# 29 semaphores instead of 48: signals between two engines share a counter, in a cached-attention decode kernel

## The chip, the cores and the metric

The kernel runs on one core of one Trainium2 chip. A time is the device time of one execution in microseconds; "before" is the median of three executions. The profile is one further execution with the hardware profiler on.

## What is computed

One decode step for two sequences (B = 2, one query each, D = 512), as a gated sum of attention and an MLP:

```
xn  = layernorm(x)                                   # x = A_x [2, 1, 512]
s   = attention(xn): q = xn @ wq (32 heads of 128), k_cache / v_cache [2, 8, 32768, 128],
      p = softmax(q.k * 128**-0.5), o = p @ v, s = o @ wo
g   = silu(B(xn)):  h = gelu(layernorm(xn) @ w1), four shifted slices of h @ w2,
      x1 = xn + (that), h2 = gelu(layernorm(x1) @ w3) @ w4, x1 + h2
out = x + s * g
```

With a sequence length of one the four shifted slices hold only padding, so w1 and w2 contribute nothing, and the kernel does not read them. What remains to be read is the K and V caches, 2 x 8 x 32768 x 128 bf16 each, 134 MB each, and some 12 MB of weights: 280.5 MB by the profile.

## The kernel before

**The work.** There are 16 *groups*, one for each sequence and KV head. A group's K and V are 8.39 MB each, laid out as 128 partitions of 256 keys. `kbuf` has three slots of half a group, `vbuf` two. For a group, VectorE transposes K in 16 pieces into the four buffers `T` (L558); TensorE multiplies each with the query matrix `z` into the score banks `sc` (L664). After eight pieces the first half of the scores is complete. VectorE takes row maxima (`mx`, `mxr`, L537 to L541), TensorE spreads them (`S`, L676), VectorE reduces them to `shift` (L569), ScalarE takes the exponential into `ep` (L478), VectorE transposes that into `pt` (L577), TensorE multiplies it with V into `o` (L687), ScalarE copies `o` to `ob` (L483). The division by the sum of a group is put off into the next group: TensorE adds up the four parts (`oT`, L624), VectorE divides (`head_on`: `den`, `rec`, `recm`, `on`, L513 to L522), TensorE turns the result (`xp`, L630), VectorE reduces it (`head_out`, L528 to L534) to `oXs`, GpSimd copies that to its place in `oX` (`put_o`, L498) and makes the next `z` (`put_z`, L491). The prologue (layernorms, q, the MLP) comes ahead of the groups; at the end come the products with `wo` (L703 to L748), `sg` = s * g (L614), `out` = x + sg (L615), and two stores (L617).

**The order.** Every engine has one queue, written out by hand. VectorE's loop body holds two groups and runs 8 turns, TensorE's holds one and runs 16, GpSimd and ScalarE have their own loops. SyncE issues all large loads in a fixed order without a loop: wq, w3, w4, K of group 0, V of group 0, then for each m the K of group m (L442), released when TensorE begins the last of the first eight pieces of group m - 1, and V of group m (L427), released when ScalarE sees the last product with V of group m - 1. After the last V come six pieces of `wo` (`wo_parts`, L457 to L466), each with a semaphore of its own (`d_wo`).

**The signals.** Outside the loops a semaphore only grows, and a `Queue` object (L27) notes which value each step waits for: `s_ve`, `s_ac`, `s_po`, `s_pe` are the engines' own counters. In the loops a signal is either *taken*, with a wait that also subtracts (`take`, L468, its row on line 469: one instruction of the sequencer), or, on VectorE, awaited as a growing count and subtracted at the end of the turn: the object `c` (`Counts`) keeps, for each semaphore, how many a turn has used, and L583 to L584 then take those totals. In front of a turn's end these are ten semaphores: `t_z`, `t_k0`, `t_used`, `t_k1`, `t_d`, `t_S`, `t_oT`, `t_xp`, `t_top`, `t_e`. `t_used` says that TensorE is done with a T buffer, `t_T` that a T piece is there, `t_mx`, `t_pt`, `t_on` that the operands of L676, L687 and L630 are there, `t_sm` and `t_oX` signal to GpSimd, `s_half`, `s_pv` release K and V loads, `s_oX` counts GpSimd's copies. An instruction carries one wait itself; a further one is a separate instruction in front of it.

**The end.** After the last store has landed, the engines meet in a barrier, GpSimd clears the range of semaphores that the program allocated (L779), and a second barrier follows. The kernel allocates 42 of the 48, the frame around it six.

Of the kernel before, what the change touches and what calls it, by code (L numbers as in the profile page):

```python
# [11 lines left out]
ALU = mybir.AluOpType  # L12
# [9 lines left out]
T_BUFS = 4  # L22
# [96 lines left out]
def kernel(  # L119
# [140 lines left out]
    d_x, d_x4, d_wq, d_w3, d_w4, d_g, d_out = (  # L260
        sem(f"d_{n}") for n in ("x", "x4", "wq", "w3", "w4", "g", "out")
    )
    d_wo = [sem(f"d_wo{i}") for i in range(len(wo_parts))]
    t_T, t_z, t_mx, t_pt, t_ob, t_on = (sem(f"t_{n}") for n in ("T", "z", "mx", "pt", "ob", "on"))
    t_used, t_top, t_e, t_S, t_oT, t_xp = (sem(f"t_{n}") for n in ("used", "top", "e", "S", "oT", "xp"))
    t_d, t_shift, t_pv, t_sm, t_oX = (sem(f"t_{n}") for n in ("d", "shift", "pv", "sm", "oX"))
    t_k = [sem(f"t_k{i}") for i in range(NPART)]
    t_v = [sem(f"t_v{i}") for i in range(NPART)]
    s_half, s_pv, s_oX = (sem(f"s_{n}") for n in ("half", "pv", "oX"))
# [19 lines left out]
    with tc.tile_critical(sync_engine=mybir.EngineType.Pool, no_gpsimd_drain=True):  # L289
# [25 lines left out]
        ve.op(lambda e: e.memset(S[:, 0:NPART * rep], 1.0), inc=(t_S, 1))  # L315
# [117 lines left out]
        load_v(0, e_h2)  # L433
        for n in range(NQ):
            sp.op(lambda v, n=n: v.dma_start(out=g4[32 * n:32 * n + B, :], in_=g[:, n * QW:(n + 1) * QW]), e_g, e_g0, inc=(d_g, 16))
# [3 lines left out]
        for m in range(1, NG):  # L439
            base = m % 2  # L440
            if m < NG - 1:
                sp.op(lambda e, m=m, base=base: e.dma_start(  # L442
                    out=kbuf[:, base * SLOT:(base + NPART) * SLOT], in_=row_view(A_k_cache, *groups[m])),
                    (s_half, m), e_q, inc=(t_k[0], 16))
            else:
                for i, h in enumerate(order(m)):
                    sp.op(lambda e, m=m, h=h, base=base: e.dma_start(
                        out=kbuf[:, (base + h) * SLOT:(base + h + 1) * SLOT],
                        in_=row_view(A_k_cache, *groups[m])[:, h * SLOT:(h + 1) * SLOT]),
                        (s_half, m), inc=(t_k[i], 16))  # L450
            load_v(m, (s_pv, m))
        for i, (a, c, r0, r1) in enumerate(wo_parts):
            cols = slice(r0 * D, r1 * D)
            if i == LOW:
                rows = wos[:, a, cols]
                for p in range(4):
                    sp.op(lambda e, p=p, rows=rows: e.dma_start(  # L457
                        out=wo_low[LQ + p:LQ + LP:4, 0:2, :],
                        in_=rows[0:2 * LP, :].rearrange("(u p) c -> p u c", u=2)[p:LP:4, :, :]), (s_pv, NG - 1), inc=(d_wo[i], 16))
                    sp.op(lambda e, p=p, rows=rows: e.dma_start(  # L460
                        out=wo_low[LQ + p:LQ + LOW_N[2]:4, 2, :], in_=rows[2 * LP + p::4, :]), (s_pv, NG - 1), inc=(d_wo[i], 16))
                continue
            if i == 0:
                sp.op(lambda e, c=c: e.dma_start(out=kbuf[:, 0:RW * D], in_=A_wo[0:128 * RW, :].rearrange("(p r) d -> p (r d)", r=RW)), (s_pv, NG - 1), inc=(d_wo[i], 16))  # L464
                continue
            sp.op(lambda e, a=a, c=c, cols=cols: e.dma_start(out=wo3[:, a:c, cols], in_=wos[:, a:c, cols]), (s_pv, NG - 1), inc=(d_wo[i], 16))  # L466
# [5 lines left out]
        ac.op(lambda v: v.activation(out=warm[:, :], in_=ones_f[:, 0:1], func=ACT.Exp), e_ones)  # L472
        with nc.Fori(0, NG // 2, engines=[ACTE]):
            for par in range(2):
                take(nc.scalar, t_shift)
                for h in range(NPART):
                    i = order(par).index(h)
                    nc.scalar.activation(  # L478
                        out=ep[i][:, :], in_=sc[i][:, :], func=ACT.Exp, scale=inv_sqrt_dh, bias=shift[:, :],
                        accum_out=rs[:, i:i + 1]).then_inc(t_e, 1)  # L480
                take(nc.scalar, t_pv)
                nc.scalar.sem_inc(s_pv, 1)  # L482
                nc.scalar.copy(out=ob[:, :], in_=o[:, :]).then_inc(t_ob, 1)  # L483

# [11 lines left out]
        def put_o(m):  # L496
            take(nc.gpsimd, t_oX)
            nc.gpsimd.tensor_copy(out=oX[:, bass.ds(m, 1), :].rearrange("p m r -> p (m r)"), in_=oXs[:, :]).then_inc(s_oX, 1)  # L498
# [5 lines left out]
        with nc.Fori(0, NG - 1, engines=[POOL]) as m:  # L504
            put_o(m)
            take(nc.gpsimd, t_sm)
            put_z(m + 1)
        put_o(NG - 1)
        e_oX = [(s_oX, m + 2) for m in range(NG - 1)] + [None]


        def head_on(c, last=False, between=None):
            nc.vector.tensor_reduce(  # L513
                out=den[:, :], in_=S[:, 0:NPART * rep].rearrange("p (i h) -> p h i", h=rep),
                axis=AX.X, op=ALU.add).wait_op(*c(t_S), "sem-ge").then_inc(*c.inc(t_d))
# [6 lines left out]
            ins = nc.vector.tensor_mul(  # L522
                out=on[:, :, :], in0=oT[:, :].unsqueeze(1).broadcast_to([128, NQ, rep]), in1=recm[:, :, :]).wait_op(*c(t_oT, 2), "sem-ge")
            if last:
                ins.then_inc(t_on, 1)

        def head_out(c, last=False):
            nc.vector.tensor_mul(  # L528
                out=xm[:, :, :], in0=xp_b[:, :].rearrange("p (r h) -> p r h", r=NQ),
                in1=mask[:, :].unsqueeze(1).broadcast_to([128, NQ, rep])).wait_op(*c(t_xp), "sem-ge").then_inc(*c.inc(t_d))  # L530
            with nc.allow_low_precision(reason="three of the four terms are zero, the fourth is bf16"):
                if last:
                    return ve.op(lambda v: v.tensor_reduce(out=oX[:, NG, :], in_=xm[:, :, :], axis=AX.X, op=ALU.add), c.at(t_d))
                nc.vector.tensor_reduce(out=oXs[:, :], in_=xm[:, :, :], axis=AX.X, op=ALU.add).wait_op(*c.at(t_d), "sem-ge").then_inc(t_oX, 1)  # L534

        def peak(c, i, *event):
# [5 lines left out]
            if i == NPART - 1:  # L542
                ins.then_inc(t_mx, 1)

        nc.br("dve_groups", engines=[DVE])
        with nc.body("dve_groups", valid_engines=[DVE]):
            c = Counts()
            for par in range(2):
                nc.vector.wait_ge(*c(t_z))
                for i, h in enumerate(order(par)):  # L550
                    u = par + h
                    kt = kbuf[:, u * SLOT:(u + 1) * SLOT].bitcast(I32)
                    for r in range(NR):
                        n = i * NR + r
                        events = ([c(t_k[i], 16)] if r == 0 else []) + ([c(t_used)] if n >= T_BUFS else [])
# [7 lines left out]
                        ins.then_inc(t_T, 1)  # L563
                        if i == 1 and r == 3:
                            peak(c, 0)
                            head_on(c)
                head_out(c)
                peak(c, 1, *c(t_used, T_BUFS))
                nc.vector.tensor_reduce(  # L569
                    out=shift[:, :], in_=S[:, NPART * rep:], axis=AX.X, op=ALU.min).wait_op(*c(t_top), "sem-ge").then_inc(t_shift, 1)  # L570
                for h in range(NPART):
                    e = c(t_e)
                    if h == NPART - 1:
                        nc.vector.tensor_mul(
                            out=sm[:, :, :], in0=sel_h[:, :].unsqueeze(1).broadcast_to([128, NPART, rep]),
                            in1=rs[:, :].unsqueeze(2).broadcast_to([128, NPART, rep])).wait_op(*e, "sem-ge").then_inc(t_sm, 1)
# [5 lines left out]
                    ins.then_inc(t_pt, 1)  # L582
# [11 lines left out]
        e_wd, e_mv, e_ws, e_s = ((pe.sem, pe.n + i) for i in (1, 2, 3, 4))  # L594
# [19 lines left out]
        e = ve.op(lambda v: v.tensor_tensor(out=sg[0:QP, :], in0=pro[0:QP, 0:QW], in1=g4[0:QP, :], op=ALU.mult), (d_g, 16 * NQ), e_s)  # L614
        e = ve.op(lambda v: v.tensor_tensor(out=out4[0:QP, :], in0=sg[0:QP, :], in1=x4_bf[0:QP, :], op=ALU.add), (d_x4, 16 * B), e)  # L615
        for b, q in ((0, sp), (1, ac)):
            q.op(lambda v, b=b: v.dma_start(out=out[b, 0, :].rearrange("(n c) -> n c", c=QW), in_=out4[b:QP:32, :]), e, inc=(d_out, 16))  # L617
        sp.wait((d_out, 32))


        def head_oT():
# [5 lines left out]
            ins.then_inc(t_oT, 1)  # L627

        def head_xp():
            nc.tensor.matmul(  # L630
                xp_b[:, :], lhsT=sel_w[:, :, :].rearrange("p j w -> p (j w)"), rhs=on[:, :, :].rearrange("p r h -> p (r h)"),
                start=True, stop=True).then_inc(t_xp, 1)
# [12 lines left out]
        pe.n, pe.seen = prologue.n, prologue.seen  # L645
# [6 lines left out]
        with nc.body("pe_groups", valid_engines=[PE]):  # L652
            for i in range(NPART):
                for r in range(NR):
                    pairs = i == 0 or r < 4
                    if not pairs:
                        take(nc.tensor, t_T)
                    elif r % 2 == 0:
                        take(nc.tensor, t_T, 2)
                    Tb = Ts[(i * NR + r) % T_BUFS][:, :].bitcast(BF16).rearrange("p (b c e) -> p b c e", b=NB, e=2)  # L660
                    zc = (NR - 1 - r) * rep
                    for nb in range(NB):
                        for w in range(2):
# [4 lines left out]
                            if i == 0 and r == NR - 1 and nb == 0 and w == 0:  # L668
                                ins.then_inc(s_half, 1)
                    ins.then_inc(t_used, 1)  # L670
# [4 lines left out]
            take(nc.tensor, t_mx)  # L675
            nc.tensor.matmul(  # L676
                S[:, NPART * rep:], lhsT=same_h[:, :], rhs=mxr[:, :, :].rearrange("p i r -> p (i r)"),
                start=True, stop=True).then_inc(t_top, 1)
            for h in range(NPART):
                fill(FILL[h])  # L680
                take(nc.tensor, t_v[h], 16)
                take(nc.tensor, t_pt)
# [13 lines left out]
                start=True, stop=True).then_inc(t_S, 1)  # L696
# [4 lines left out]
        with nc.body("pe_output", valid_engines=[PE]):  # L701
# [7 lines left out]
            take(nc.tensor, t_on)  # L709
            head_xp()  # L710
            for i in (0, 2, LOW, 3, 4, 5):
# [13 lines left out]
                for k in range(a, c):  # L725
                    pe.wait(e_oX[(B - 1) * Hkv + k], (d_wo[i], 16 * (8 if i == LOW else 1)), *((e_low, e_low0) if i == LOW else (e_wide,) if i == 0 else ()))
# [57 lines left out]
```

## Time and profile before

| | |
|---|---|
| three executions | 656.88, 657.32, 658.47 us; median 657.32 us |
| profiled execution, its own time | 656.51 us |
| span, first to last instruction | 654.7 us |
| TensorE, matmul | 431.4 us busy, 66% |
| VectorE | 379.5 us, 58% |
| ScalarE / GpSimd | 39.7 us / 14.2 us, 6% / 2% |
| DMA queue of SyncE | 280.50 MB, 99.1% of 16 engines' span |

"PE" is TensorE, "PEld" its weight load, "DVE" VectorE, "ACT" ScalarE, "POOL" GpSimd, "SP" SyncE; a name with q is that engine's sequencer. The span is the time from the first to the last instruction; the 1.81 us by which the execution's own time is longer lie around it. Semaphore instructions do not count as busy, but they appear as rows of a line.

### The profile page before, as it was taken

The page shows a single profiled execution, that of the slowest core. Times are in us where ns is not written, and L with a number is a line of the kernel's source. Part 1 is how long each engine was busy: PE and PEld are TensorE (multiplying, and loading weights), DVE is VectorE, ACT ScalarE, POOL GpSimd, SP SyncE. Part 2 cuts the span into 40 slices and gives each one's busy share as a digit, 9 for nine tenths or more (in the row PEclk, how much of TensorE's full clock was granted, in tenths as well). Part 3 has the DMA queues.
Part 4 walks back from the last instruction along what each step waited for, and adds up shares of the span by engine and source line. Part 5 has one row for each costly group of instructions (what it writes and reads, how often), then busy time and mean ns, then how long its engine had stood idle before and what let it go on. Part 6 is the DMA issues. An engine that isn't in the chain of part 4 may idle for free. (4 is left out here: it accounts for less than half of the span.)

```text
span 654.7 us, 6536 instructions
## 1 busy us (share of the span) xinstructions
PE 431.4 (66%) x2568; PEld 163.6 (25%) x2568; DVE 379.5 (58%) x538; ACT 39.7 (6%) x90; POOL 14.2 (2%) x45
## 2 busy tenths in 40 slices
PE   2438487583958748395783839668384875838886
PEld 0013132231313213131321313222131322313332
DVE  5348193673919457292855819276481936639681
ACT  1200001000010100001000000100001010000100
POOL 1200000000000000000000000000000000000000
PEclk9759789696997969789796978969697796969999
DMA  8999999999999999999999999999999999998997
GB/s 366 435 449 449 445 392 445 440 448 396 444 440 448 440 400 444 444 448 392 448 440 448 416 424 444 444 448 392 448 440 448 416 424 444 444 448 388 448 416 292
DMA packets 6314, 280.54 MB, mean 428 GB/s; under 512 B 798, under 2 KB 936, under 8 KB 1448
## 3 DMA queue, kind: packets, MB, share of 16 engines
q1 hardware_dynamic: 6300, 280.50, 99.1%
q8 instruction: 2, 0.03, 0.0%
q10 hardware_dynamic: 12, 0.00, 0.0%
HBM read 280.50 MB, written 0.00 MB: 428 GB/s over the span
## 5 line engine op out<-in xcount | busy, mean ns | idle before, releaser
L558 DVE STREAM_TRANSPOSE T<-kbuf 128x1024 int32<-128x1024 int32 x256 | 294.8, 1211 | 202.9 <-DMA kbuf<-in_A_k_cache_dram 196.3
L664 PE MATMUL sc<-T,z 128*128 128x512 bf16 x1024 | 277.7, 420 | 176.1 <-PEq L469 172.7
L664 PEld LDWEIGHTS sc<-T,z 128*128 128x128 bf16 x1024 | 98.0, 104 | 339.4 <-issue 258.8
L687 PE MATMUL o<-vbuf,pt 128*16 128x512 bf16 x1024 | 78.8, 380 | 7.3 <-PEq L469 4.4
L637 PE MATMUL pro<-ob,comb 128*2 128x512 f32 x130 | 61.1, 592 | 0.0
L478 ACT ACTIVATE ep<-sc,shift 128x512 bf16<-128x512 f32 x32 | 21.7, 682 | 485.5 <-ACTq L469 485.5
L687 PEld LDWEIGHTS o<-vbuf,pt 128*16 128x16 bf16 x1024 | 27.2, 88 | 55.3 <-issue 33.2
L577 DVE STREAM_TRANSPOSE pt<-ep 128x512 bf16<-128x512 bf16 x32 | 22.7, 708 | 15.0 <-ACT ep L478 15.0
L537 DVE TENSOR_REDUCE mx<-sc 128x1 f32<-128x512 f32 x32 | 21.5, 672 | 15.8 <-PE sc L664 15.8
L676 PE MATMUL S<-mxr,same_h 128*128 128x64 f32 x32 | 6.5, 285 | 18.4 <-PEq L469 18.4
L624 PEld LDWEIGHTS oT<-sel_o,ob 128*128 128x128 f32 x136 | 17.7, 191 | 3.2 <-issue 0.5
L637 PEld LDWEIGHTS pro<-ob,comb 128*2 128x2 f32 x130 | 9.6, 84 | 26.8 <-issue 21.9
L624 PE MATMUL oT<-sel_o,ob 128*128 128x4 f32 x136 | 16.2, 242 | 0.0
L483 ACT COPY ob<-o 128x512 f32<-128x512 f32 x16 | 9.4, 585 | 96.4 <-ACTq L469 96.4
L498 POOL COPY oX<-oXs 128x4 bf16 (+1 forms) x16 | 3.0, 186 | 527.5 <-POOLq L469 527.5
L676 PEld LDWEIGHTS S<-mxr,same_h 128*128 128x128 f32 x32 | 4.8, 188 | 26.2 <-issue 26.2
L569 DVE TENSOR_REDUCE shift<-S 128x1 f32<-128x64 f32 x16 | 3.6, 224 | 9.4 <-PE S L676 9.4
L541 DVE TENSOR_SCALAR mxr<-row_of,mx 128x32 f32<-128x32 f32 x32 | 7.7, 242 | 1.1
L694 PEld LDWEIGHTS S<-sm,ones_f 128*128 128x128 f32 x32 | 5.0, 195 | 6.9 <-issue 6.9
L491 POOL TENSOR_TENSOR z<-qr,quad 128x64 bf16<-128x64 bf16 x16 | 4.7, 293 | 80.6 <-POOLq L469 65.6
L694 PE MATMUL S<-sm,ones_f 128*128 128x8 f32 x32 | 6.4, 273 | 0.0
L372 PE MATMUL qrb<-ident,xs_bf 34*128 34x34 bf16 x4 | 0.3, 193 | 9.1 <-DVE xs_bf L337 9.1
(103 smaller groups left out, 82.0 us busy)
## 6 DMA issues: line engine op xcount, KB each, us to landing
kbuf<-in_A_k_cache_dram SPq DMA_DIRECT2D x2, 4096.0 KB, 22.6
vbuf<-in_A_v_cache_dram SPq DMA_DIRECT2D x2, 4096.0 KB, 22.5
kbuf<-in_A_wq_dram SPq DMA_DIRECT2D x1, 4096.0 KB, 12.3
vbuf<-in_B_w_dram SPq DMA_DIRECT2D x2, 1792.0 KB, 17.9
kbuf<-in_A_wo_dram SPq DMA_DIRECT2D x1, 2048.0 KB, 31.5
kbuf<-in_A_wo_dram SPq DMA_DIRECT2D x3, 512.0 KB, 26.3
shared<-in_A_wo_dram SPq DMA_DIRECT2D x4, 66.0 KB
kbuf<-in_A_k_cache_dram SPq DMA_DIRECT2D x15, 27.4
```

The costliest lines, as they stand in the source:

```text
L478: nc.scalar.activation(out=ep[i][:, :], in_=sc[i][:, :], func=ACT.Exp, scale=inv_sqrt_dh, bias=shift[:, :], accum_out=rs[:, i:i + 1]).then ...
L483: nc.scalar.copy(out=ob[:, :], in_=o[:, :]).then_inc(t_ob, 1)
L537: ins = nc.vector.tensor_reduce(out=mx[:, i:i + 1], in_=sc[i][:, :], axis=AX.X, op=ALU.max)
L541: ins = nc.vector.tensor_scalar_mul(out=mxr[:, i, :], in0=row_of[:, :], scalar1=mx[:, i:i + 1]).wait_op(*c.at(t_d), "sem-ge")
L558: ins = nc.vector.transpose(out=Ts[n % T_BUFS][:, :].rearrange("p (b t k) -> p t b k", b=NB, t=RT), in_=kt[:, r * W:(r + 1) * W].rearrange ...
L577: ins = nc.vector.transpose(out=pt[h][:, :, :].rearrange("p r (t h) -> p t r h", h=rep), in_=ep[order(par).index(h)][:, :].rearrange("p (t ...
L624: ins = nc.tensor.matmul(oT[:, :], lhsT=ob[:, t * Dh:(t + 1) * Dh], rhs=sel_o[:, t, :], start=(t == 0), stop=(t == VT - 1))
L637: nc.tensor.matmul(pro[0:B, :], lhsT=comb[:, :], rhs=ob[:, :], start=True, stop=True)
L664: ins = nc.tensor.matmul(sc[i][:, :], lhsT=z[:, nb, w, zc:zc + 128], rhs=Tb[:, nb, :, w], start=(r == 0 and nb == 0 and w == 0), stop=(r = ...
L676: nc.tensor.matmul(S[:, NPART * rep:], lhsT=same_h[:, :], rhs=mxr[:, :, :].rearrange("p i r -> p (i r)"), start=True, stop=True).then_inc( ...
L687: ins = nc.tensor.matmul(o[32 * j:32 * j + VT * rep, :], lhsT=pt[h][:, r, a * VT * rep:(a + 1) * VT * rep], rhs=vt[:, u * VT:(u + 1) * VT, ...
L694: nc.tensor.matmul(S[:, 0:NPART * rep], lhsT=ones_f[:, :], rhs=sm[:, :, :].rearrange("p i h -> p (i h)"), start=True, stop=True).then_inc( ...
```

## The change

The same signals are carried by fewer counters; every computing instruction, load and store stays, in the same order.

- VectorE to TensorE: `t_T`, `t_mx`, `t_pt`, `t_on` become `t_vt`. VectorE to GpSimd: `t_sm`, `t_oX` become `t_vg`.
- TensorE to VectorE: `t_used`, `t_top`, `t_S`, `t_oT`, `t_xp` become `t_tv`. A group has 20 such signals in a fixed order, and VectorE waits for places in it (`used`, `sum_of`, `out_of`, `turned`); a turn's end subtracts 40.
- `recm`, which signalled `t_oT` beside TensorE, signals `t_d`, so that `on` now has two waits, one of them separate.
- `s_half`, `s_pv`, `s_oX` become further counts of `s_pe`, `s_ac`, `s_po`; `s_sp`, which nothing used, goes.
- The six `wo` pieces and the stores count on in the prologue's `d_wq`, `d_w3`, `d_w4`, `d_x`, `d_x4`, `d_g`.

A turn's end on VectorE now subtracts six semaphores: `t_z`, `t_k0`, `t_k1`, `t_d`, `t_e`, `t_tv`.

```diff
-    sp = Queue(nc.sync, sem("s_sp"))
+    sp = Queue(nc.sync, None)
...
+    d_wo = [d_wq, d_w3, d_w4, d_x, d_x4, d_g]
+    n_wo = [16, 16, 16, 16, 16 * B, 16 * NQ]
+    for i in range(len(wo_parts)):
+        n_wo[i] += 16 * (8 if i == LOW else 1)
+    d_out, n_out = d_wq, n_wo[0] + 16 * B
+    t_vt, t_vg, t_tv = (sem(f"t_{n}") for n in ("vt", "vg", "tv"))
+    t_z, t_ob, t_e, t_d, t_shift, t_pv = (sem(f"t_{n}") for n in ("z", "ob", "e", "d", "shift", "pv"))
...
-                    (s_half, m), e_q, inc=(t_k[0], 16))
+                    (pe.sem, pe_0 + m), e_q, inc=(t_k[0], 16))
...
-            load_v(m, (s_pv, m))
+            load_v(m, (ac.sem, ac_0 + m))
...
-        ac.op(lambda v: v.activation(out=warm[:, :], in_=ones_f[:, 0:1], func=ACT.Exp), e_ones)
+        ac.op(lambda v: v.activation(out=warm[:, :], in_=ones_f[:, 0:1], func=ACT.Exp), e_ones, inc=False)
...
+        N_T = NPART * NR + 4
+        def used(par, n):
+            return t_tv, par * N_T + n + 2 + (n >= NR) + (n >= NR + 5)
+        def sum_of(par):
+            return t_tv, par * N_T + 1
+        def out_of(par, last=False):
+            return t_tv, par * N_T + (2 if last else NR + 2)
+        def turned(par, last=False):
+            return t_tv, par * N_T + (3 if last else NR + 8)
...
-                in1=sel_h[:, :].unsqueeze(2).broadcast_to([128, NQ, rep])).wait_op(*c.at(t_d), "sem-ge").then_inc(t_oT, 1)
+                in1=sel_h[:, :].unsqueeze(2).broadcast_to([128, NQ, rep])).wait_op(*c.at(t_d), "sem-ge").then_inc(*c.inc(t_d))
+            e = c.at(t_d)
             if between:
                 between()
+            nc.vector.wait_ge(*out_of(par, last))
             ins = nc.vector.tensor_mul(
-                out=on[:, :, :], in0=oT[:, :].unsqueeze(1).broadcast_to([128, NQ, rep]), in1=recm[:, :, :]).wait_op(*c(t_oT, 2), "sem-ge")
+                out=on[:, :, :], in0=oT[:, :].unsqueeze(1).broadcast_to([128, NQ, rep]), in1=recm[:, :, :]).wait_op(*e, "sem-ge")
...
-                        events = ([c(t_k[i], 16)] if r == 0 else []) + ([c(t_used)] if n >= T_BUFS else [])
+                        events = ([c(t_k[i], 16)] if r == 0 else []) + ([used(par, n - T_BUFS)] if n >= T_BUFS else [])
...
+            c(t_tv, 2 * N_T)
             for s_, n in c.totals():
                 take(nc.vector, s_, n)
...
-        e = ve.op(lambda v: v.tensor_tensor(out=sg[0:QP, :], in0=pro[0:QP, 0:QW], in1=g4[0:QP, :], op=ALU.mult), (d_g, 16 * NQ), e_s)
+        e = ve.op(lambda v: v.tensor_tensor(out=sg[0:QP, :], in0=pro[0:QP, 0:QW], in1=g4[0:QP, :], op=ALU.mult), (d_g, n_wo[-1]), e_s)
...
-        sp.wait((d_out, 32))
+        sp.wait((d_out, n_out))
...
-                        take(nc.tensor, t_T)
+                        take(nc.tensor, t_vt)
```

More of the change, by code (lines that the diff above doesn't have):

```diff
@@ L259 @@
     pe = LateQueue(nc.tensor, sem("s_pe"))
[L260 to L266, printed above, removed]
+    d_wq, d_w3, d_w4, d_x, d_x4, d_g = (sem(f"d_{n}") for n in ("wq", "w3", "w4", "x", "x4", "g"))
+    d_wo = [d_wq, d_w3, d_w4, d_x, d_x4, d_g]
+    assert len(d_wo) == len(wo_parts)
+    n_wo = [16, 16, 16, 16, 16 * B, 16 * NQ]
[4 more added lines that the diff above has]
+    t_z, t_ob, t_e, t_d, t_shift, t_pv = (sem(f"t_{n}") for n in ("z", "ob", "e", "d", "shift", "pv"))
     t_k = [sem(f"t_k{i}") for i in range(NPART)]
     t_v = [sem(f"t_v{i}") for i in range(NPART)]
-    s_half, s_pv, s_oX = (sem(f"s_{n}") for n in ("half", "pv", "oX"))
     kbuf_wq = kbuf[:, 2 * SLOT:3 * SLOT]
@@ L314 @@
         ve.op(lambda e: e.memset(o[:, :], 0.0))
-        ve.op(lambda e: e.memset(S[:, 0:NPART * rep], 1.0), inc=(t_S, 1))
+        ve.op(lambda e: e.memset(S[:, 0:NPART * rep], 1.0), inc=(t_tv, 1))
         ve.op(lambda e: e.memset(pro[:, :], 0.0))
@@ L496, in put_o @@
         def put_o(m):
-            take(nc.gpsimd, t_oX)
-            nc.gpsimd.tensor_copy(out=oX[:, bass.ds(m, 1), :].rearrange("p m r -> p (m r)"), in_=oXs[:, :]).then_inc(s_oX, 1)
+            take(nc.gpsimd, t_vg)
+            nc.gpsimd.tensor_copy(out=oX[:, bass.ds(m, 1), :].rearrange("p m r -> p (m r)"), in_=oXs[:, :]).then_inc(po.sem, 1)
         po.wait(e_qr, e_z0, e_quad)
@@ L505, with head_on @@
             put_o(m)
-            take(nc.gpsimd, t_sm)
+            take(nc.gpsimd, t_vg)
             put_z(m + 1)
         put_o(NG - 1)
-        e_oX = [(s_oX, m + 2) for m in range(NG - 1)] + [None]
-        def head_on(c, last=False, between=None):
+        e_oX = [(po.sem, po.n + m + 2) for m in range(NG - 1)] + [None]
+        po.n += NG
+        N_T = NPART * NR + 4
[7 more added lines that the diff above has]
+            return t_tv, par * N_T + (3 if last else NR + 8)
+        def head_on(c, par=0, last=False, between=None):
             nc.vector.tensor_reduce(
                 out=den[:, :], in_=S[:, 0:NPART * rep].rearrange("p (i h) -> p h i", h=rep),
-                axis=AX.X, op=ALU.add).wait_op(*c(t_S), "sem-ge").then_inc(*c.inc(t_d))
+                axis=AX.X, op=ALU.add).wait_op(*sum_of(par), "sem-ge").then_inc(*c.inc(t_d))
             nc.vector.reciprocal(out=rec[:, :], in_=den[:, :]).wait_op(*c.at(t_d), "sem-ge").then_inc(*c.inc(t_d))
@@ L533, in head_out @@
                     return ve.op(lambda v: v.tensor_reduce(out=oX[:, NG, :], in_=xm[:, :, :], axis=AX.X, op=ALU.add), c.at(t_d))
-                nc.vector.tensor_reduce(out=oXs[:, :], in_=xm[:, :, :], axis=AX.X, op=ALU.add).wait_op(*c.at(t_d), "sem-ge").then_inc(t_oX, 1)
+                nc.vector.tensor_reduce(out=oXs[:, :], in_=xm[:, :, :], axis=AX.X, op=ALU.add).wait_op(*c.at(t_d), "sem-ge").then_inc(t_vg, 1)
         def peak(c, i, *event):
@@ L542, in peak @@
             if i == NPART - 1:
-                ins.then_inc(t_mx, 1)
+                ins.then_inc(t_vt, 1)
         nc.br("dve_groups", engines=[DVE])
@@ L562 @@
                             ins.wait_op(*e, "sem-ge")
-                        ins.then_inc(t_T, 1)
+                        ins.then_inc(t_vt, 1)
                         if i == 1 and r == 3:
                             peak(c, 0)
-                            head_on(c)
-                head_out(c)
-                peak(c, 1, *c(t_used, T_BUFS))
+                            head_on(c, par)
+                head_out(c, par)
+                peak(c, 1, *used(par, NT - 1))
                 nc.vector.tensor_reduce(
-                    out=shift[:, :], in_=S[:, NPART * rep:], axis=AX.X, op=ALU.min).wait_op(*c(t_top), "sem-ge").then_inc(t_shift, 1)
+                    out=shift[:, :], in_=S[:, NPART * rep:], axis=AX.X, op=ALU.min).wait_op(t_tv, (par + 1) * N_T, "sem-ge").then_inc(t_shift, 1)
                 for h in range(NPART):
@@ L581 @@
                         ins.wait_op(*e, "sem-ge")
-                    ins.then_inc(t_pt, 1)
+                    ins.then_inc(t_vt, 1)
+            c(t_tv, 2 * N_T)
             for s_, n in c.totals():
@@ L626, in head_oT @@
                     start=(t == 0), stop=(t == VT - 1))
-            ins.then_inc(t_oT, 1)
+            ins.then_inc(t_tv, 1)
         def head_xp():
@@ L644 @@
         prologue, pe = pe, Queue(nc.tensor, pe.sem)
-        pe.n, pe.seen = prologue.n, prologue.seen
+        pe.n, pe.seen = prologue.n + NG, prologue.seen
+        assert prologue.n == pe_0
         turn = nc.alloc_registers("turn", engines=[PE])
@@ L656 @@
                     if not pairs:
-                        take(nc.tensor, t_T)
+                        take(nc.tensor, t_vt)
                     elif r % 2 == 0:
-                        take(nc.tensor, t_T, 2)
+                        take(nc.tensor, t_vt, 2)
                     Tb = Ts[(i * NR + r) % T_BUFS][:, :].bitcast(BF16).rearrange("p (b c e) -> p b c e", b=NB, e=2)
@@ L668 @@
                             if i == 0 and r == NR - 1 and nb == 0 and w == 0:
-                                ins.then_inc(s_half, 1)
-                    ins.then_inc(t_used, 1)
+                                ins.then_inc(pe.sem, 1)
+                    ins.then_inc(t_tv, 1)
                     if i == 1 and r == 4:
@@ L674 @@
                     head_oT()
-            take(nc.tensor, t_mx)
+            take(nc.tensor, t_vt)
             nc.tensor.matmul(
                 S[:, NPART * rep:], lhsT=same_h[:, :], rhs=mxr[:, :, :].rearrange("p i r -> p (i r)"),
-                start=True, stop=True).then_inc(t_top, 1)
+                start=True, stop=True).then_inc(t_tv, 1)
             for h in range(NPART):
@@ L681 @@
                 take(nc.tensor, t_v[h], 16)
-                take(nc.tensor, t_pt)
+                take(nc.tensor, t_vt)
                 vt = vbuf[:, h * SLOT:(h + 1) * SLOT].rearrange("p (t d) -> p t d", d=Dh)
@@ L708 @@
             fill(1)
-            take(nc.tensor, t_on)
+            take(nc.tensor, t_vt)
             head_xp()
@@ L725 @@
                 for k in range(a, c):
-                    pe.wait(e_oX[(B - 1) * Hkv + k], (d_wo[i], 16 * (8 if i == LOW else 1)), *((e_low, e_low0) if i == LOW else (e_wide,) if i == 0 else ()))
+                    pe.wait(e_oX[(B - 1) * Hkv + k], (d_wo[i], n_wo[i]), *((e_low, e_low0) if i == LOW else (e_wide,) if i == 0 else ()))
                     for r in range(r0, r1):
```

31 lines of the change are left out of this document (17 added, 14 removed).

## The prediction, made before the changed kernel had run

> **What bounds the kernel now.** I read the page first: which engine is full, and whether the transfers ever pause.
>
> ```profile
> span 654.7 us, 6536 instructions
> PE 431.4 (66%) x2568; PEld 163.6 (25%) x2568; DVE 379.5 (58%) x538; ACT 39.7 (6%) x90; POOL 14.2 (2%) x45
> ...
> DMA  8999999999999999999999999999999999998997
> ...
> q1 hardware_dynamic: 6300, 280.50, 99.1%
> ```
>
> No compute engine is over 66% busy, while SyncE's one DMA queue fills 99.1% of the 16 engines' span. The shares are averages, so the second view is the table by stretches. Its last two columns are the DMA share and the GB/s.
>
> ```profile
> 0.00:1.84 1.84, 0.00 (x0) 0.00 (x0) 0.65 (x3) 0.34 (x1) 0.91 (x7) 1.00 0.00 0
> 1.84:80.00 78.16, 36.72 (x216) 12.79 (x216) 37.07 (x73) 8.28 (x14) 6.44 (x10) 0.83 1.02 435
> 80.00:160.00 80.00, 51.38 (x298) 19.61 (x298) 46.68 (x62) 4.06 (x10) 0.96 (x4) 0.84 1.00 432
> 320.00:400.00 80.00, 54.32 (x309) 20.64 (x308) 47.46 (x63) 4.06 (x10) 0.96 (x4) 0.85 1.00 433
> 560.00:640.00 80.00, 60.46 (x361) 22.46 (x360) 53.43 (x79) 5.51 (x14) 1.14 (x5) 0.94 0.99 429
> 640.00:650.25 10.25, 9.04 (x135) 3.86 (x132) 1.79 (x9) 1.17 (x2) 0.00 (x0) 1.00 0.94 387
> 650.25:654.70 4.45, 0.53 (x20) 0.30 (x20) 0.58 (x2) 0.00 (x0) 0.00 (x0) 0.94 0.00 0
> ```
>
> The reader is to see three parts: 1.84 us before data moves, 648.4 us in which the DMA engines are full (0.94 at the least), and 4.45 us after the last weight has landed. Only the first and the third can be shortened by fewer signals; the middle moves 280.5 MB at some 433 GB/s whatever the semaphores do, as long as its queue never runs dry. The chain that ended last and the waits (microseconds in total, times, longest) agree:
>
> ```profile
> 623.13 27.11 DMA kbuf<-in_A_wo_dram
> 650.24 0.04 issue
> 650.28 0.56 PE pro L748 x20
> 650.84 0.02 issue
> 650.86 0.30 DVE sg L614
> 651.16 0.02 issue
> 651.19 0.29 DVE out L615
> ```
>
> ```profile
> DVE T L558 <- DMA kbuf<-in_A_k_cache_dram: 196.3, 17, 14.4
> PE pro L748 <- DMA kbuf<-in_A_wo_dram: 0.8, 1, 0.8
> SPq L591 <- DMA out_dram<-out: 1.2, 1, 1.2
> ```
>
> VectorE stands 196.3 us, 11.5 us per wait, until K has landed: it is ahead of the data in every group. At the end TensorE waits 0.8 us for the last piece of wo.
>
> How far is the queue from running dry? From issue to landing (last number, us):
>
> ```profile
> kbuf<-in_A_k_cache_dram SPq DMA_DIRECT2D x15, 27.4
> vbuf<-in_A_v_cache_dram SPq DMA_DIRECT2D x15, 27.2
> ```
>
> One group of K or V is 128 x 32768 bf16, 8.39 MB, or 19.4 us at 433 GB/s. So each load is issued 27.2 - 19.4 = 7.8 us before its turn: that is the cover. A signal that releases a load may come 7.8 us later in a group before one DMA engine idles.
>
> **The change, part by part.** The loads keep their order and sizes, and every matmul, transpose and activation stays. SyncE's K loads now wait on TensorE's main counter instead of s_half, the V and wo loads on ScalarE's instead of s_pv. The same instruction gives the signal at the same place, with the prologue's count added, and the warm-up activation no longer counts, so the totals fit. Cost nothing; if the cover of 7.8 us were gone, a late signal would cost its own lateness.
>
> The takes (a wait that also subtracts) all stand on line 469. This view gives minimum, median and maximum in ns; PEldq, DVEq and POOLq are sequencers:
>
> ```profile
> L469 PEldq EVENT_SEMAPHORE  x258: 51/51/51, 43.4 to 645.8; - x129
> L469 DVEq EVENT_SEMAPHORE  x80: 21/21/21, 105.9 to 638.6; - x80
> L469 POOLq EVENT_SEMAPHORE  x31: 17/17/17, 61.3 to 633.2; - x31
> ```
>
> *TensorE's and GpSimd's takes.* T, mx, pt and on become one counter t_vt, sm and oX one counter t_vg. VectorE produces these in the very order in which TensorE, or GpSimd, takes them, and both are in-order queues, so no take can pass on the wrong event or wait for a later one. The number of takes is unchanged: the 51 ns of TensorE's and 17 ns of GpSimd's stay as they are. Nothing.
>
> The timeline around the last group, with the idle time before an instruction and its releaser in brackets:
>
> ```profile
> 638.84 0.36 DVE L591 TENSOR_TENSOR T<-oX,sel_h 128x64 bf16<-128x64 bf16 x2 [0.49 <-DVEq L469]
> 644.57 1.03 PE L624 MATMUL oT<-sel_o,ob 128*128 128x4 f32 x8
> 645.63 0.17 DVE L522 TENSOR_TENSOR on<-oT,recm 128x16 bf16<-128x16 f32 x1 [0.45 <-PE oT L624]
> ```
>
> *VectorE's takes.* used, oT, xp, top and S become t_tv, of which VectorE awaits absolute places in a 20-step round per group. TensorE reaches the awaited step at the same instruction as before: S, counted ahead of a group's first used, is earlier in TensorE's queue anyway. At the end of each of the 8 turns VectorE subtracts 6 counters instead of 10, so 80 rows become 48: 32 fewer at 21 ns is 0.67 us of sequencer time, at most 8 x 0.5 us by the idle time before L591, which is all that the ten together cost behind the last turn. Behind these instructions stands the next T transpose, which then waits 11.5 us for K. The gain on the path is nothing in the loop; after the last turn it is behind the 0.8 us wait for wo.
>
> *The added wait in head_on.* The product on used to carry one wait for a counter that recm and oT shared. Now a separate wait for oT goes ahead of it, 17 times. Behind it are queued on and, in 16 groups, four T transposes on which TensorE waits. Its price is 21 ns from below (the DVEq row) and 0.49 us from above (the idle behind ten such waits); ten such instructions shared that idle time, 0.05 us each, so I take twice this, 0.1 us, for the wait and for handing on the product behind it: nearer to the lower end, since its own row is 21 ns. In 16 groups 0.1 us goes into the cover of 7.8 us. In the last one, on at 645.63 starts some 0.1 us later, xp and the products after it too, and TensorE then waits 0.7 instead of 0.8 us for wo. Nothing on the path; without that slack, 0.1 us (0.02 to 0.49).
>
> *Late loads on old counters.* The first user of a shared counter, the last of the prologue's loads (g4, on d_g) and the first wo piece, from the timeline of SyncE:
>
> ```profile
> 0.89 0.38 SPq L291 DMA_DIRECT2D kbuf<-in_A_wq_dram  x1
> 29.24 1.28 SPq L435 DMA_DIRECT2D g<-g  x2
> 614.80 0.43 SPq L464 DMA_DIRECT2D kbuf<-in_A_wo_dram  x1
> ```
>
> The six wo pieces count on in d_wq, d_w3, d_w4, d_x, d_x4 and d_g. Before sg, VectorE awaits d_g. That wait was over some 600 us earlier; now its number includes the last wo piece, which lands at 650.24. Behind it are queued sg and out, and the store waits for those. But sg also waits for TensorE's last product, at 650.84, 0.6 us later, so 0.1 us to release and dispatch is hidden; from above, 0.49 us is hidden too. The wait of out on d_x4 concerns a piece that landed earlier. The output counts on in d_wq; SyncE awaits 64 instead of 32, released by the same two stores. Nothing.
>
> [...]
>
> *The clear at the end.* The one edit that lies on the path is not in the diff's lines: the program ends by clearing the range of semaphores that it allocated, on GpSimd alone, between two barriers after everything else.
>
> ```profile
> L779 POOLq EVENT_SEMAPHORE_RANGE_CLEAR  x1: 291/291/291, 654.1 to 654.1; - x1
> ```
>
> It clears 48 (42 of the listing, 6 of the frame around it), that is 6.1 ns each, if it goes by the number; 29 would take 176 ns. Gain 0.115 us, between 0 (a fixed price) and 0.291 us.
>
> The sum: -0.115 us, everything else under cover. Against the profiled execution: 656.51 us of its own, of which 654.7 us are the span and 1.81 us lie around it; it becomes 656.4. It ran 0.81 us (0.12%) faster than the median of the three runs, 657.32; with the same shift the median becomes 657.2.
>
> [...]
>
> **The rivals.**
>
> *Faster outside the span.* If what lies around the span also goes by the allocated semaphores, at most 1.81 x 19/48 = 0.72 us goes, and 0.115 in the span: 656.5 us. Nothing in the trace shows it. Chance 0.06; even so it is within 0.3%.
>
> *The signals set the pace after all, faster.* If VectorE's turn ends were on the path, 32 dropped takes at 0.05 us each (0.49 over ten) bring 1.6 us, and at most 8 x 0.49 = 3.9: 653.4 to 655.6. Against it: 11.5 us of waiting for K in each group. Chance 0.03.
>
> *Slower: the separate wait in head_on.* It stands in the middle of a group with four T transposes behind it. If it held VectorE for the upper price each time and these were on the path, 17 x 0.49 = 8.3 us: 665.6. It decides only once it delays a load's release by over 7.8 us in one group, sixteen times its upper price. For it: the wait is an instruction of its own on the engine's sequencer, as the rows of line 469 show such ones. Against it: the DMA share of 1.00. Chance 0.03.
>
> *It brings nothing at all.* If the clear has a fixed price, or the after-runs only repeat the spread, the time is 657.3. Chance 0.08, the same side as the forecast.
>
> **How the numbers follow.** About 0.3%, 2 us, is what a measurement of this kernel can tell from no change: the three runs alone span 656.88 to 658.47. The forecast, 657.2 us, has 0.80. The four cases above have 0.20. The forecast, the first rival and the last lie within 0.3% of before (0.94); from that I take 0.02 to each side for a median that falls otherwise, which leaves 0.90. Faster is 0.03 + 0.02 = 0.05, slower 0.03 + 0.02 = 0.05. For the range: the four times seen, 656.51 to 658.47, less 0.1, give 656.4 to 658.4; below, the bounds of the reset add 0.4; above, one such wait at its upper price adds 0.49: 656.0 to 658.9.
>
> **What would show it.** Right: the DMA share stays at 1.00 from 1.84 us to about 650, K and V still land some 27 us after issue, the last wo piece lands within 1 us of 650.2, VectorE has 48 takes, the clear takes about 176 ns, and the stretch after the last landing is 4.3 instead of 4.45 us. Wrong: a slice of DMA under 0.9 before 640 us, an issue-to-landing time near 19 us (the cover gone), VectorE idle behind the new wait and not behind K, sg starting more than 0.1 us behind the last product, or a clear of 291 ns.

## The result and the profile after

The changed kernel took 656.50 us (median of 22 executions, 656.11 to 657.57) against 657.47 us (22, 656.44 to 658.47): a ratio of 0.9987, interval 0.9981 to 0.9993. It is faster by 0.13%, inside the 0.3% that the prediction called no change, but by more than the 0.115 us forecast. The profiled execution took 656.46 us (before 656.51), its span 654.4 us (before 654.7).

The page, the stretches and the chain of the changed kernel, with the columns as before:

```profile
span 654.4 us, 6521 instructions
...
DMA  8999999999999999999999999999999999998997
...
q1 hardware_dynamic: 6300, 280.50, 99.1%
```

```profile
1.84:80.00 78.16, 39.44 (x216) 13.30 (x216) 37.21 (x73) 8.29 (x14) 6.44 (x10) 0.85 1.02 435
80.00:160.00 80.00, 52.05 (x298) 19.84 (x298) 46.90 (x62) 4.07 (x10) 0.96 (x4) 0.84 1.00 432
320.00:400.00 80.00, 54.91 (x309) 20.96 (x307) 47.60 (x63) 4.07 (x10) 0.96 (x4) 0.85 1.00 433
560.00:640.00 80.00, 61.11 (x360) 22.70 (x358) 53.40 (x76) 5.51 (x14) 1.15 (x5) 0.91 0.98 424
640.00:650.04 10.04, 8.97 (x139) 3.94 (x137) 1.79 (x9) 1.17 (x2) 0.00 (x0) 1.00 0.95 393
650.04:654.40 4.36, 0.54 (x20) 0.29 (x20) 0.58 (x2) 0.00 (x0) 0.00 (x0) 0.87 0.00 0
```

```profile
623.82 26.16 DMA kbuf<-in_A_wo_dram
649.98 0.04 issue
650.03 0.58 PE pro L775 x20
650.61 0.02 issue
650.63 0.30 DVE sg L640
```

The transfers fill the same stretch at the same rate (within 6 GB/s in every window), and the last piece of wo ends it again, 0.2 us earlier in this execution. The stretch behind it is 4.36 us instead of 4.45. Of one row there, the clear, the difference of 0.09 us is seen: it was 291 ns. Beside it stand VectorE's takes, 48 instead of 80:

```profile
L806 POOLq EVENT_SEMAPHORE_RANGE_CLEAR  x1: 200/200/200, 653.9 to 653.9; - x1
```

```profile
L473 DVEq EVENT_SEMAPHORE  x48: 21/21/21, 105.7 to 638.1; - x48
```

So one execution shows 0.09 us behind the last landing, and the comparison 0.97 us between medians. The experiments ask where the rest comes from, and whether the cover held that the prediction rested on.

### The profile page after: what moved, and what is told of

The parts are those of the page before. It is cut to its first block, busy times and chain, and to the rows that moved or that the text cites. A ratio compares the mean times of both kernels' runs of the same rounds, so it can differ in the third digit from the quotient of the medians.

```text
span 654.4 us, 6521 instructions
## 1 busy us (share of the span) xinstructions
PE 436.4 (67%) x2568; PEld 165.2 (25%) x2568; DVE 380.0 (58%) x538; ACT 39.7 (6%) x90; POOL 14.3 (2%) x45
## 3 DMA queue, kind: packets, MB, share of 16 engines
q1 hardware_dynamic: 6300, 280.50, 99.1%
## 5 line engine op out<-in xcount | busy, mean ns | idle before, releaser
L691 PE MATMUL sc<-T,z 128*128 128x512 bf16 x1024 | 280.9, 424 | 171.7 <-PEq L473 168.5
L691 PEld LDWEIGHTS sc<-T,z 128*128 128x128 bf16 x1024 | 99.4, 105 | 336.9 <-issue 257.2
L714 PEld LDWEIGHTS o<-vbuf,pt 128*16 128x16 bf16 x1024 | 27.2, 88 | 54.8 <-issue 32.7
L421 PE MATMUL sc<-vbuf,h_bf 128*2 128x512 bf16 x14 | 4.9, 524 | 2.4 <-DVE h_bf L418 2.4
## 6 DMA issues: line engine op xcount, KB each, us to landing
kbuf<-in_A_k_cache_dram SPq DMA_DIRECT2D x15, 27.3
```

The source lines that it names most:

```text
L691: ins = nc.tensor.matmul(sc[i][:, :], lhsT=z[:, nb, w, zc:zc + 128], rhs=Tb[:, nb, :, w], start=(r == 0 and nb == 0 and w == 0), stop=(r = ...
L714: ins = nc.tensor.matmul(o[32 * j:32 * j + VT * rep, :], lhsT=pt[h][:, r, a * VT * rep:(a + 1) * VT * rep], rhs=vt[:, u * VT:(u + 1) * VT, ...
```

## The experiments

**The number of semaphores alone.** The changed kernel with 19 unused ones:

```diff
     t_v = [sem(f"t_v{i}") for i in range(NPART)]
+    unused = [sem(f"u{i}") for i in range(19)]
```

> The changed kernel with 19 more semaphores allocated and never used, so that the clear at the end covers 48 again; nothing else differs. Theory A (the clear and whatever else goes by the number allocated make the gain): the clear takes 291 ns again, the gain of 0.97 us is lost, ratio to before 1.000. Theory B (the clear is 0.09 us, and the rest of the gain comes from how the waits and signals stand in the program): clear 291 ns, ratio about 0.9988, some 0.1 us slower than the changed kernel. Theory C (the rest is chance in the DMA engines' stalls): anything from 0.998 to 1.001 with an interval that holds 1.

Measured: 0.9995 (0.9986 to 1.0004), mean 657.02 us. The interval holds the ratios of theories A and B both. In the same way 100 unused ones went into the kernel before:

> The kernel before with 100 unused semaphores more, 148 in the clear. By the two clears seen (291 ns for 48, 200 ns for 29: 4.8 ns each and 61 ns fixed) it takes 770 ns, and the span grows by 0.48 us. Theory A (something outside the span goes by the number too): the time grows by more than 0.48 us, up to 0.48 + 1.81 x 100/48 = 4.3 us, and the time minus span is over 1.9 us. Theory B: ratio 1.0007, time minus span stays at 1.8 us.

Measured: 1.0002 (0.9993 to 1.0011), fastest execution 656.93 us, 0.66 above the fastest of before in that comparison. The clears, of the changed kernel padded to 48 and of before with 148, each with GpSimd's drains at the end of the program (the longest of the three, the last number of 34/41/..., stands just ahead of the clear):

```profile
L807 POOLq DRAIN  x3: 34/41/114, 653.5 to 654.2; - x3
L807 POOLq EVENT_SEMAPHORE_RANGE_CLEAR  x1: 291/291/291, 653.9 to 653.9; - x1
```

```profile
L780 POOLq DRAIN  x3: 34/41/260, 653.9 to 655.3; - x3
L780 POOLq EVENT_SEMAPHORE_RANGE_CLEAR  x1: 832/832/832, 654.4 to 654.4; - x1
```

The clear goes by the number: 291 ns for 48 whatever else is in the program, then 5.4 ns for each one more. The drain ahead of it goes with the number too: 99 ns in every profile with 29 semaphores, 114 ns in every one with 48, 260 ns with 148. Clear and drain together grew by 0.69 us with 100 more, which is the 0.66 us of the fastest executions. Nothing outside the span grows: with 100 more, the time around it is 1.95 us in the mean, against 1.98 for before in the same comparison. Theory A is out as a price per semaphore.

**The two halves.** In one, only the loads and the release signals share counters (`d_wo`, `s_half`, `s_pv`, `s_oX`); in the other, only the loops do (`t_vt`, `t_vg`, `t_tv`, six takes, the separate wait). Unused semaphores bring both to 48:

```diff
+    unused = [sem(f"u{i}") for i in range(11)]      # loads alone
...
+    unused = [sem(f"u{i}") for i in range(8)]       # loops alone
```

> Half of the change: the wo pieces and the stores count on in the prologue's load counters, and s_half, s_pv, s_oX count on in the engines' own; the loop counters stay as before, VectorE takes ten at a turn's end and on keeps its one wait. Padded to 48 semaphores, so the clear is as before (291 ns). Theory B1 (the rest of the gain lies in the release of the loads): ratio 0.9988, as for the whole change without its clear. Theory B2 (it lies in VectorE's loop): 1.000. Theory C: no order between this and the other half, both hold 1.

> The other half: t_vt, t_vg, t_tv in the loops, six takes at a turn's end and the separate wait in head_on; the loads and s_half, s_pv, s_oX as before. Padded to 48, clear 291 ns. Theory B1 (the release of the loads makes the rest of the gain): ratio 1.000. Theory B2 (VectorE's loop makes it): 0.9988. Theory C: holds 1.

Measured: loads 1.0002 (0.9993 to 1.0011), loops 0.9997 (0.9988 to 1.0006). Neither repeats the gain, as theory C has it.

**No change, and the change again.**

> The changed kernel unaltered, a second time, on the chip of this call. Theory B (the change itself brings some 0.9 us): ratio 0.9987 again, most executions near 656.5 us where before has them near 657.5. Theory C (a fixed gain of 0.1 to 0.2 us, the rest chance in how often an execution falls into the upper of two clusters, 656.5 and 657.6 us): ratio between 0.9987 and 0.9998, with the fastest execution 0.1 to 0.3 us under the fastest of before.

> The kernel before, unaltered, compared with itself: what the comparison makes of no change at all. Both theories: 1.000. If it comes out 0.0005 or more from 1.000, a ratio of 0.9995 for a half of the change says nothing, and theory C gains.

Measured: the changed kernel 0.9996 (0.9987 to 1.0004), before against itself 1.0000 (0.9991 to 1.0008). The comparison shows no bias of its own; the first ratio of the changed kernel, 0.9987, lies at the edge of the interval of its repetition. The fastest executions, 656.32 and 656.36 us, are 0.04 us apart.

**How much cover there is.** Waits that are already over, put ahead of `on` in the changed kernel's loop:

```diff
             nc.vector.wait_ge(*out_of(par, last))
+            for _ in range(0 if last else 20):          # and 100
+                nc.vector.wait_ge(*out_of(par, last))
```

> The changed kernel with twenty further copies of the separate wait in head_on, in the 16 groups of the loop and not in the tail; all are over when they are reached. Forecast (hidden under a cover of 7.8 us): at 0.02 to 0.49 us each they take 0.4 to 9.8 us of VectorE in a group, probably 20 x 0.1 = 2 us, on starts that much later behind recm, V is issued 2 us later, and the time stays at 656.5 us, ratio to before 0.9987 to 1.000. The rival (VectorE's signals on the path): 16 x 2 = 32 us slower, 689 us.

Measured: 0.9990 (0.9981 to 0.9999). The waits cost VectorE less than expected. The timeline with 20 of them, and with 100, and the line of the waits themselves in the latter (duration ns, least, median, most):

```profile
599.19 0.17 DVE L540 TENSOR_TENSOR recm<-rec,sel_h 128x16 f32<-128x16 f32 x1
600.25 0.17 DVE L549 TENSOR_TENSOR on<-oT,recm 128x16 bf16<-128x16 f32 x1 [0.88 <-DVE recm L540]
```

```profile
335.23 0.17 DVE L540 TENSOR_TENSOR recm<-rec,sel_h 128x16 f32<-128x16 f32 x1
340.35 0.17 DVE L549 TENSOR_TENSOR on<-oT,recm 128x16 bf16<-128x16 f32 x1 [4.94 <-issue]
```

```profile
L548 DVEq EVENT_SEMAPHORE  x816: 21/50/50, 57.8 to 647.0; - x164
```

From recm to on it is 1.06 us with 20 extra and 5.12 with 100, against 0.21 without: 0.04 to 0.05 us each. With 20, the 0.85 us that VectorE lost in each group were hidden, as forecast.

> The same with a hundred copies: some 11 us in a group if one is 0.11 us, over the cover of 7.8 us. Forecast: V is released 11 us later in a group, its issue-to-landing falls to about 19.4 us, the DMA engines idle some 3 us in each of 15 groups, and the time is about 656 + 15 x 3 = 700 us. If the time stays, the cover is larger than the prediction worked out; if it rises by 16 x 11 = 176 us, there was none.

Measured: 676.24 and 679.60 us, a ratio of 1.0312 (1.0286 to 1.0339), less than the forecast of 700, since a wait cost half of what was taken (0.05 us for 0.11). Issue to landing and the stretches of this kernel:

```profile
vbuf<-in_A_v_cache_dram SPq DMA_DIRECT2D x15, 22.0
```

```profile
80.00:160.00 80.00, 55.87 (x298) 21.19 (x298) 45.27 (x60) 4.06 (x10) 0.96 (x4) 0.83 0.99 420
320.00:400.00 80.00, 55.34 (x298) 21.04 (x298) 46.52 (x62) 4.06 (x10) 0.96 (x4) 0.84 0.98 422
...
663.81:674.00 10.19, 6.20 (x120) 3.36 (x119) 2.37 (x11) 1.17 (x2) 0.00 (x0) 0.87 0.00 0
```

V's time to landing fell from 27.1 to 22.0 us, by about what VectorE lost. Yet 4.9 us of delay, under the 7.8 us that were to cover it, cost 20 us: the rate in the groups fell from 433 to 421 GB/s in these two stretches, which moved the last landing from 650.0 to 663.8 us, and the tail grew from 4.4 to 10.2 us, since the last group's own arithmetic now ends behind the last weight (the chain has its `o` products until 663.96 us). The cover is over 0.85 us and under 4.9.

The packets in the traces say where it ended. Here are the issues of V for the same group in the changed kernel and in the one with 100 waits:

```profile
189.02 0.33 SPq L430 DMA_DIRECT2D vbuf<-in_A_v_cache_dram  x1
```

```profile
199.74 0.33 SPq L430 DMA_DIRECT2D vbuf<-in_A_v_cache_dram  x1
```

The packets can be sorted into 16 engines by putting each to the one whose packet before ended there. In the changed kernel the first engine then begins with this V at 194.74, 5.7 us after the issue, and the last at 196.53. With 100 waits no packet was in flight at 200.5, and the first of V began at 200.69, 0.95 us after its issue. So the queue ran dry, and 0.95 us is the time that this load took to start. From here on it goes like this for V of every second group (0.95 to 0.97 us); in the groups between, the first packet begins 2.3 to 2.4 us after the issue. The changed kernel has 5.3 to 6.2 us there (only 4.0 for V of group 1). Less the 0.95 us, an estimate of what the first engine can spare is 4.3 to 5.3 us.

**The same again, for the mean.** Ratios of some 11 executions are known to about 0.001, the size of the effect. One further comparison repeated three kernels beside the changed one:

> The changed kernel padded to 48 semaphores, a second time, beside the changed kernel itself in the same call. So far, means over executions: before 657.4 us, changed 656.8, padded 657.0. If the clear alone parts the two (theory B), the padded one is 0.09 us slower than the changed one. If the number allocated makes the whole gain (theory A), it is 0.6 us slower, as slow as before. The standard error of the difference over all executions will be about 0.17 us, so the two can be told apart.

> The half with the loads on old counters, padded to 48, a second time. First time its mean was 657.4 us, as before. Theory B1 (this half makes the rest of the gain): mean 656.9 us. Theory B2 or C: 657.4 us again.

> The half with the shared loop counters, padded to 48, a second time. First time its mean was 657.2 us, 0.2 under before, with a standard error of 0.2. Theory B2 (VectorE's loop makes the rest of the gain): mean 656.9 us. Theory B1 or C: 657.4 us.

> The changed kernel a third time, as the neighbour of the other three. Theory B: mean 656.7 us or less, 0.6 under before. Theory C: nearer to before, 657.2 us.

Measured: padded 1.0003 (0.9994 to 1.0012), loads 1.0003 (0.9992 to 1.0013), loops 0.9999 (0.9991 to 1.0008), changed 0.9993 (0.9982 to 1.0004). The means are 657.41, 657.35, 657.24 and 656.96 us. The halves came out as theory C has it; the padded kernel, 0.45 ± 0.25 us above the changed one, decides neither for A (0.6) nor for B (0.09). All executions together, with the standard error of the mean; the last two columns cover those whose span is known (109 of before):

| kernel | executions | mean us | span less clear, mean / least | around the span, mean | over 2.2 us |
|---|---|---|---|---|---|
| before | 131 | 657.32 ± 0.06 | 654.93 / 654.1 | 2.06 | 28 of 109 |
| changed | 46 | 656.81 ± 0.08 | 654.71 / 654.1 | 1.90 | 0 of 46 |
| changed, padded to 48 | 23 | 657.22 ± 0.13 | 655.01 / 654.1 | 1.92 | 1 of 23 |
| loads alone, 48 | 23 | 657.39 ± 0.14 | 655.08 / 654.3 | 2.02 | 5 of 23 |
| loops alone, 48 | 23 | 657.24 ± 0.11 | 654.99 / 654.1 | 1.96 | 2 of 23 |
| before and 100 unused | 11 | 657.60 ± 0.18 | 654.82 / 654.3 | 1.95 | 1 of 11 |

The gain over all executions is 0.51 ± 0.10 us. But it is not the same in the three comparisons that have the changed kernel beside before (the second and third on different chips, the first on one not on record; the second counts before's own repetition with before). The last two columns are before less changed; the spans of before are not on record for the first:

| comparison | before, us | changed, us | gain, us | gain in span less clear | gain around the span |
|---|---|---|---|---|---|
| first | 657.49 ± 0.14 (22) | 656.61 ± 0.08 (22) | 0.88 ± 0.17 | - | - |
| second | 657.38 ± 0.09 (41) | 657.04 ± 0.15 (12) | 0.34 ± 0.18 | 0.07 ± 0.17 | 0.18 ± 0.05 |
| third | 657.16 ± 0.14 (35) | 656.96 ± 0.19 (12) | 0.20 ± 0.24 | -0.12 ± 0.19 | 0.23 ± 0.08 |

The two repetitions together give 0.28 ± 0.14 us: 0.09 us is the clear, seen in every profile, 0.20 ± 0.05 us lies around the span, and in the rest of the span there is nothing, -0.01 ± 0.13 us.

Around the span, kernels with the old loops are over 2.2 us in 34 of 143 executions, those with the shared loop counters (with the 20 waits' 0 of 10) in 3 of 102; the run with 100 waits, 1 of 2, is left out. At 48 semaphores it is 33 of 132 against 3 of 46. So this part goes with the loop half of the change, not with the number. What fills that time shows in the transfers of some profiled executions after their last instruction, in the window from 655 to 660 us. The loads half, with 2.47 us around its span, and before against itself, with 2.28:

```profile
q8 instruction: 1, 0.02, 1.8%
```

```profile
q8 instruction: 1, 0.02, 1.7%
```

One block of instructions (one packet, 0.02 MB) was fetched there. All four profiled executions with over 2.2 us have such a transfer; of the other ten, at 1.75 to 2.06 us, only one does. In these five the traces show the end of the fetch 2.2 to 2.8 us behind the last instruction, and the time around the span is 0.2 to 0.3 us less than that each time. Three of the five are kernels with the shared loop counters (of nine profiled), two have the old loops (of five), so the profiles do not show the fetch to be rarer with shared counters; why long times are, stays open.

What the whole 0.51 us has beyond clear and fetch, some 0.26 us, rests on the first comparison alone. The least span without the clear is the same 654.1 us, so nothing fixed has gone beyond that. The changed kernel lay over half a microsecond above its least span in 6 of 22 executions there, but in 15 of 24 in the repetitions, against 69 of 109 for before; its own span less the clear was 654.50 ± 0.08 us there and 654.90 ± 0.11 later. The experiments were made because the first gain was large, so it is no fair sample, and neither half nor the padded kernel shows a shorter span. Whether chance or the first comparison's chip made it, no run tells. None of the profiled executions lies clearly in the upper group, so that no trace shows what the longer ones hold.

## Why the prediction was right, and where it was not

*The bound* held: the transfers end the kernel after as before, the DMA share stays at 0.98 to 1.02 up to 640 us, K and V land 27.3 and 27.1 us after issue (27.4 and 27.2 before), and 20 extra waits on VectorE in each group, where the change adds one, cost nothing.

*The clear* with its drain was the one fixed gain, 0.106 us for 0.115 forecast. The clear alone gave 0.091; the term was mis-sized because it was priced through zero: with 29, 48 and 148 semaphores it took 200, 291 and 832 ns, that is 4.8 ns each from 29 to 48, which leaves some 60 ns fixed, and 5.4 ns each from 48 to 148. The 15 ns of the drain were not in the sum, so part of the nearness is luck.

*The sum* failed at "everything else under cover", as far as it took the time around the span for constant. The repetitions gained 0.28 us, 0.20 of it there. The first rival named that place and gave 656.5 us, which the first comparison hit, but that was luck: its cause is refuted, since 100 semaphores more left the time around the span as it was (1.95 us with 148, 1.98 with 48). What differs there goes with the loops' program, and is a late fetch of instructions where it was seen. What else fills that time, no run shows.

*The separate wait* was taken at 0.1 us, between 0.02 and 0.49. In the changed kernel's loop it is nothing at all:

```profile
599.40 0.18 DVE L540 TENSOR_TENSOR recm<-rec,sel_h 128x16 f32<-128x16 f32 x1
599.61 0.17 DVE L547 TENSOR_TENSOR on<-oT,recm 128x16 bf16<-128x16 f32 x1
```

0.21 us apart, as before (598.71 and 598.92). In the tail, where it really waits, on starts 1.14 us behind oT instead of 1.06. The forecast was that xp and the products after it would move too, and that TensorE's wait for wo would take this up. That step was wrong. Before, and then changed:

```profile
644.57 1.03 PE L624 MATMUL oT<-sel_o,ob 128*128 128x4 f32 x8
645.52 1.02 PE L637 MATMUL pro<-ob,comb 128*2 128x512 f32 x2
646.48 0.18 PE L630 MATMUL xp<-on,sel_w 128*128 128x16 bf16 x1
...
650.28 0.53 PE L748 MATMUL pro<-kbuf,oX 128*2 128x128 bf16 x20 [0.81 <-DMA kbuf<-in_A_wo_dram]
```

```profile
644.51 1.02 PE L650 MATMUL oT<-sel_o,ob 128*128 128x4 f32 x8
645.46 1.02 PE L663 MATMUL pro<-ob,comb 128*2 128x512 f32 x2
646.42 0.18 PE L656 MATMUL xp<-on,sel_w 128*128 128x16 bf16 x1
...
650.03 0.56 PE L775 MATMUL pro<-kbuf,oX 128*2 128x128 bf16 x20 [0.63 <-DMA kbuf<-in_A_wo_dram]
```

```profile
645.65 0.17 DVE L547 TENSOR_TENSOR on<-oT,recm 128x16 bf16<-128x16 f32 x1 [0.52 <-PE oT L650]
```

TensorE has two other products (pro) between oT and xp, and xp starts 1.91 us behind oT in both kernels: the 0.08 us went no further than these products. TensorE waits 0.63 instead of 0.81 us for wo because the last piece landed 0.2 us earlier in this execution. "Nothing on the path" was right, for another reason than the one given.

*The takes* became 48 and the idle time of 0.49 us at the end of the last turn went, with nothing gained on the path. The price of 0.05 us each, ten into 0.49, was too low: in both traces they start 0.11 us apart, and the first of the ten began while the transposes before them still ran. *The late loads:* sg, which now waits for the last wo piece too, starts 0.02 us behind the last product, as before.

*The cover* of 7.8 us was mis-sized, though the change never came near it. The step took the time to landing, which is that of the last of 16 engines, less the transfer's own time, and called all of it usable. But the first engine was free 1.6 to 1.8 us before the last, and a load on the dry queue needed 0.95 us from issue to first packet; what is left is 4.3 to 5.3 us, and 4.9 us of delay used it up in every second group; the kernel, its longer tail included, took 3% more. The slower rival's point of decision, 7.8 us in a group, was set too high with it.

*The range:* its lower end counts 0.4 us for "the bounds of the reset", and no run shows such a term: the runs showed the clear, 0.200 us with 29 semaphores and 0.291 with 48, and around the span a time that did not grow with their number (1.95 us with 148, 1.98 with 48). The bounds of the clear, 0 and 0.291 us, give 0.18 us more than the forecast's 0.115, and 656.2 as the lower end; 656.50 lies inside either.

## What to carry to other kernels

While the transfers never paused (99.1% of 16 engines' span, in the changed kernel and with 20 extra waits), signals that moved VectorE by tenths of a microsecond were free (0.85 us in each group with those waits), and the place to look for a gain is what stands alone at the end, such as the clear, which took 4.8 to 5.4 ns for each further semaphore allocated. Issue-to-landing time less the transfer's own time was an upper bound of the cover, not the cover (7.8 us here, where the first engine could spare 4.3 to 5.3); delay one engine on purpose to measure it. A gain of a tenth of a per cent needs dozens of executions on both sides, the kernel compared with itself, each half tried at an equal number of semaphores, and a repetition that is judged without the comparison that raised the question.

## What the runs showed of the hardware

A wait that was already over cost VectorE nothing when one stood ahead of a small instruction (0.21 us from start to start with it, in the changed kernel, and without it, in the one before), and 0.04 to 0.05 us each when 20 or 100 stood in a row. Takes started 0.11 us apart on VectorE at the last turn's end of both kernels, though each row is 21 ns long. After the last instruction of some executions a block of instructions was still fetched (5 of 14 profiled), and the time around the span was then 2.01 to 2.60 us, without it 1.75 to 2.06. On a queue that had run dry, with 100 waits, the first packet of V began 0.95 to 0.97 us after its issue. The clear of semaphores at the program's end and the drain ahead of it grew with the number allocated: 200 and 99 ns for 29, 291 and 114 ns for 48, 832 and 260 ns for 148.
